# Re-cutting the head of a fused attention and GeGLU kernel: one 256-column part, 512-column dummies, an earlier T3 copy, and later loads for chunk 2

## The chip, the cores and the metric

The kernel runs on one core of a Trainium2 chip. The metric is the device time of one execution in microseconds (us); medians over several executions are quoted.

## The reference

```python
def reference(A_x, A_k_cache, A_v_cache, A_wq, A_wo, B_x, B_w_gate, B_w_up, B_w_down):
    xn = _layernorm(A_x)                       # 2048 x 448, bf16
    q  = xn @ A_wq                             # 16 heads of 256
    p  = softmax(q k^T / 16)                   # last 512 rows of the caches, 8 KV heads
    s  = (p v) @ A_wo
    g  = silu((gelu(xn @ B_w_gate) * (xn @ B_w_up)) @ B_w_down)   # F = 1792
    return A_x + s * g
```

## The kernel before

Each of five engines (PE the matmul engine, ACT, DVE, POOL, and SP for transfers) runs its own list of operations. A semaphore is a counter by which one engine tells another that a step is done; a small planner derives the waits for them. Each matmul is two PE instructions, the load of its weights (PEld in the traces) and the matmul itself, so 9 matmuls fewer are 18 PE instructions fewer. The tokens are handled in chunks of 512 columns; each chunk has four tiles of 128 tokens. A "unit" is one block of 128 columns of the gate and up matrices, for one chunk; it holds two PSUM banks (parts of the memory that PE writes to). The steady loop does two units per step, from unit 4 on.

The head is the part until the loop runs. A tile must be loaded, normalised (statistics on DVE, square root on ACT, scaling on DVE) and transposed on PE into `xnT` before any unit can use it. The first chunk's tiles come one after the other, so the head computes units 0 to 2 in parts of 128 columns, a part for each tile as it arrives.

```python
        warm(19, 2)                 # 19 dummy matmuls of 256 columns, ahead of the first tile
        ln_first(0)                 # statistics and square root
        ln_first(1)
        ln_second(0)                # reciprocal and scaling
        ln_tp_pe(0, ((0, 6), (1, 4)))   # T0: PE transposes of tile 0, copies to xnT by ACT
        warm(2, 2)
        ln_second(1, "act")
        HEAD, PH = (0, 1, 2), (0, 2, 4)
        T = ((None, 6),)
        ln_first(2)                 # on ACT, tile 2's square root stands ahead of T1's copy
        gu_group(HEAD, PH, (0, 1), ((0, 0),))
        ln_tp_pe(1, T)              # T1
        gu_group(HEAD, PH, (0, 1), ((0, 1), 1))
        ...
        ln_tp_pe(2, T)              # T2
        ...
        gu_group(HEAD[:1], PH[:1], (2, 3), (0,))
        ln_a()                      # statistics of tile 4
        ln_tp_pe(3, T, "dve")       # T3, copied by DVE
        ln_a()                      # statistics of tile 5
        ln_b()                      # scaling of tile 4, then its transpose by DMA
        gu_group(HEAD[1:], PH[1:], (2, 3), (0,))
        gu_group(HEAD, PH, (2, 3), (1,))
        gu_group(HEAD[:2], PH[:2], (3, 4))
        for ph in range(2):
            gu_group((3,), (6,), None, (ph,))          # unit 3, all 512 columns
            gu_group(HEAD[2:], PH[2:], (3, 4), (ph,))  # unit 2, last 128 columns
```

`gu_group(units, banks, part, phases)` writes columns `part` (in tiles) of these units. Two matmuls on 64 rows each run side by side, as a pair (in the trace of the kernel before, two of 128 columns start 0.002 to 0.020 us apart and each lasts about 0.22): 8 matmuls in phase 0 and 6 in phase 1 per unit.

The planner orders the waits of an operation by the index of the operation waited for, the largest first; and the emitter issues them in that order ahead of the operation's first instruction.

```python
            for key, d in sorted(want.items(), key=lambda kv: -kv[1].idx):
                ...
                o.waits.append(d)
        ...
    def emit(self, name, eng):
        for o in self.per[name]:
            for d in o.waits:
                eng.wait_ge(...)
            ins = o.fn(eng)
```

The softmax here doesn't subtract the row's maximum and nothing guards it: scores larger than these inputs give would overflow.

## Time and profile before

| kernel before | |
|---|---|
| median of the first 3 runs | 556.48 us (556.04 to 556.8) |
| span of the profiled run | 554.7 us |
| PE busy | 547.6 us, 99% |
| granted PE clock | 1.000 |

The first fence is from the page of the kernel before: the engines' busy times, the queue of instruction transfers (packets, MB, share), and the chain of work that ended last, by engine.

```profile
PE 547.6 (99%) x3626; PEld 260.6 (47%) x3651; DVE 317.1 (57%) x817; ACT 274.1 (49%) x727; POOL 32.9 (6%) x64
...
q8 instruction: 29, 0.48, 0.4%
...
PE 97%; DMA 1%; ACT 1%; issue 0%; DVE 0%; SPq 0%
```

PE is the bound. There is no other engine to relieve, so with the same matmuls time can be won only where PE stands still. The next fence shows where: the busy time of each engine in two stretches of the kernel before (length, then busy us and instructions per engine, granted clock, DMA share, GB/s).

```profile
5.00:14.00 9.00, 8.37 (x220) 6.33 (x220) 7.49 (x23) 5.28 (x12) 1.70 (x4) 1.00 1.09 359
14.00:38.00 24.00, 24.00 (x228) 10.65 (x222) 18.97 (x44) 9.78 (x17) 4.75 (x12) 1.00 0.60 148
```

From 14 to 38 us PE is never idle; before that it is. A matmul's end is modelled in this trace, and matmuls overlap, so the busy time understates small stops. The distance from one matmul's start to the next is the better ruler, and this document uses it: "lost" is that distance less what the same matmuls need where they run without a stop. That need is measured: in the kernel before pairs of 128 columns start 0.056 us apart and pairs of 512 columns 0.216. The 256-column dummies start 0.213 us apart until about 4.8 us, then 0.110. The granted clock of the page does not show this change of pace (`--windows` gives 1.00 from 0 to 5 us too), so "slow" and "fast" pace of PE are read here from the starts alone.

The largest stop is shown by the PE timeline of the kernel before (start, us from first start to last modelled end, tile, shape, count, idle time before it):

```profile
12.25 0.40 PE L328 MATMUL bank<-xnT,wgur 64*128 64x512 bf16 x2
12.47 0.29 PE L328 MATMUL bank<-xnT,wgu 64*128 64x128 bf16 x4
12.99 0.23 PE L328 MATMUL bank<-xnT,wgu 64*128 64x128 bf16 x2 [0.23 <-issue]
13.06 0.22 PE L328 MATMUL bank<-xnT,wgur 64*128 64x128 bf16 x2
```

The lines at 12.47 and 12.99 belong to one group of eight matmuls. By single starts the stop runs from 12.543 to 12.994: 0.451 us where 0.056 is needed, so 0.395 lost. "issue" means that no wait is seen. The matmul after the stop is the 452nd PE instruction in the trace, with weight loads and waits that are instructions of their own counted too; its pair's two weight loads, the 450th and 451st, are held up with it.

These are lines of the engines' timelines of the kernel before, DVE and ACT, then the weight loads that follow:

```profile
6.17 0.63 DVE L376 BATCH_NORM_STATS2 stats<-x 128x6 f32<-128x448 bf16 x1
...
7.05 0.30 ACT L392 ACTIVATE ve<-mv,epst 128x1 f32<-128x1 f32 x1 [0.54 <-DVE mv L379]
7.25 0.58 ACT L322 ACTIVATE xnT<-bank 128x512 bf16<-128x512 bf16 x1
...
7.88 0.17 PEld L328 LDWEIGHTS bank<-xnT,wgu 64*128 64x128 bf16 x6 [0.23 <-ACT xnT L322]
```

ACT takes tile 2's square root (7.05) ahead of T1's copy (7.25), so PE's restart at 7.888 hangs on tile 2's statistics at 6.17, and these on the arrival of tile 2's x, which landed at 6.151. T3's copy stands on DVE behind tile 4's statistics (the first line is their last step):

```profile
10.06 0.18 DVE L379 BATCH_NORM_AGGREGATE mv<-stats 128x2 f32<-128x6 f32 x1
...
10.16 0.39 DVE L438 COPY xnT<-bank 128x512 bf16<-128x512 bf16 x1
```

### The profile page before, as it was taken

The page shows a single profiled execution, that of the slowest core. Times are in us where ns is not written, and L with a number is a line of the kernel's source. Part 1 is how long each engine was busy: PE and PEld are TensorE (multiplying, and loading weights), DVE is VectorE, ACT ScalarE, POOL GpSimd, SP SyncE. Part 2 cuts the span into 40 slices and gives each one's busy share as a digit, 9 for nine tenths or more (in the row PEclk, how much of TensorE's full clock was granted, in tenths as well). Part 3 has the DMA queues.
Part 4 walks back from the last instruction along what each step waited for, and adds up shares of the span by engine and source line. Part 5 has one row for each costly group of instructions (what it writes and reads, how often), then busy time and mean ns, then how long its engine had stood idle before and what let it go on. Part 6 is the DMA issues. An engine that isn't in the chain of part 4 may idle for free.

```text
span 554.7 us, 9768 instructions
## 1 busy us (share of the span) xinstructions
PE 547.6 (99%) x3626; PEld 260.6 (47%) x3651; DVE 317.1 (57%) x817; ACT 274.1 (49%) x727; POOL 32.9 (6%) x64
## 2 busy tenths in 40 slices
PE   8999999999999999999999999999999999999997
PEld 6444444444544444554444444544444454444455
DVE  6783534443385588326588745258747625758722
ACT  5432324353485588205588735058747505758600
POOL 1120830000000000000000000000000000000000
PEclk9999999999999999999999999999999999999999
DMA  9460699401174087413086804147704713807601
GB/s 294 112 164 9 201 283 320 77 1 39 38 133 97 5 152 154 87 35 92 1 151 154 153 1 77 34 106 153 146 11 95 134 34 90 152 20 152 153 8 34
DMA packets 163599, 57.63 MB, mean 104 GB/s; under 512 B 151456, under 2 KB 160672, under 8 KB 163552
## 3 DMA queue, kind: packets, MB, share of 16 engines
q1 hardware_dynamic: 159488, 45.16, 38.7%
q0 software_dynamic: 3296, 11.27, 6.7%
q8 instruction: 29, 0.48, 0.4%
q10 hardware_dynamic: 768, 0.57, 0.3%
q14 instruction: 18, 0.15, 0.1%
HBM read 17.92 MB, written 1.84 MB: 36 GB/s over the span
## 4 chain that ended last, share of the span: by engine, by line
PE 97%; DMA 1%; ACT 1%; issue 0%; DVE 0%; SPq 0%
PE bank L328 97%; DMA x<-in_A_x_dram 1%; ACT qT L322 1%; SPq L316 0%; DVE stats L376 0%; ACT xnT L322 0%; DVE tmp L679 0%; ACT ve L392 0%; DVE ofin L682 0%; PE bank L427 0%; DVE mv L379 0%
## 5 line engine op out<-in xcount | busy, mean ns | idle before, releaser
L641 ACT ACTIVATE p<-bank 128x512 f32<-128x512 f32 x256 | 149.5, 597 | 102.9 <-PE bank L328 100.6
L645 DVE TENSOR_SCALAR pn<-p,rden 128x512 bf16<-128x512 f32 x256 | 124.5, 486 | 16.9 <-DMA pT<-pn 8.1
L328 PE MATMUL bank<-pT,va 128*128 128x512 bf16 x512 | 120.8, 379 | 0.0
L328 PE MATMUL bank<-kT,qT 128*128 128x512 bf16 x487 | 117.8, 379 | 2.0 <-ACT qT L322 1.0
L328 PE MATMUL bank<-wo,oT 128*128 128x448 bf16 (+2 forms) x544 | 97.8, 341 | 0.0
L328 PE MATMUL bank<-xnT,wq 64*128 64x512 bf16 x768 | 94.4, 376 | 0.0
L328 PE MATMUL bank<-xnT,wgu 64*128 64x512 bf16 (+1 forms) x780 | 83.6, 347 | 0.4 <-issue 0.2
L328 PEld LDWEIGHTS bank<-pT,va 128*128 128x128 bf16 x512 | 50.0, 98 | 60.5 <-DMA pT<-pn 0.7
L328 PEld LDWEIGHTS bank<-kT,qT 128*128 128x128 bf16 x512 | 49.6, 98 | 61.2 <-issue 2.5
L328 PEld LDWEIGHTS bank<-wo,oT 128*128 128x128 bf16 x544 | 52.0, 98 | 45.5
L628 DVE CAST qT<-bank 128x512 bf16<-128x512 f32 x64 | 42.9, 692 | 51.0 <-PE bank L328 51.0
L322 ACT ACTIVATE qT<-bank 128x512 bf16<-128x512 f32 x64 | 38.2, 597 | 60.6 <-PE bank L328 59.0
L328 PEld LDWEIGHTS bank<-xnT,wq 64*128 64x128 bf16 x768 | 37.0, 94 | 46.4 <-ACT p L641 1.7
L322 ACT ACTIVATE gl<-bank 128x512 bf16<-128x512 f32 x56 | 33.1, 597 | 49.7 <-PE bank L328 46.5
L495 DVE TENSOR_TENSOR actT<-bank,gl 128x512 bf16<-128x512 f32 x56 | 37.8, 690 | 33.8 <-PE bank L328 25.3
L328 PEld LDWEIGHTS bank<-xnT,wgu 64*128 64x128 bf16 x780 | 35.3, 94 | 39.0 <-issue 1.1
L641 ACT ACTIVATION_READ_ACCUMULATOR p<-bank 128x1 f32 x256 | 52.8, 206 | 0.0
L644 DVE RECIPROCAL rden<-rsum 128x1 f32<-128x1 f32 x256 | 40.4, 158 | 20.3 <-ACT p L641 20.0
L679 DVE SCALAR_TENSOR_TENSOR tmp<-bank,g 128x448 f32<-128x448 f32 (+2 forms) x17 | 10.2, 597 | 71.3 <-PE bank L328 71.3
L664 DVE CAST oT<-bank 128x512 bf16<-128x512 f32 x64 | 43.8, 684 | 6.9 <-PE bank L328 6.9
L328 PE MATMUL bank<-wd,actT 128*128 128x448 bf16 x224 | 43.0, 353 | 0.0
L322 ACT ACTIVATE oT<-bank 128x512 bf16<-128x512 f32 x64 | 39.2, 612 | 7.0 <-PE bank L328 7.0
(39 smaller groups left out, 184.1 us busy)
## 6 DMA issues: line engine op xcount, KB each, us to landing
wo<-in_A_wo_dram POOLq DMA_DIRECT2D x4, 896.0 KB, 18.5
wq<-in_A_wq_dram POOLq DMA_DIRECT2D x2, 1536.0 KB, 10.0
va<-in_A_v_cache_dram POOLq DMA_DIRECT2D x8, 256.0 KB, 13.4
pT<-pn SPq DMA_TRANSPOSE x128, 2.8
xr<-in_A_x_dram POOLq DMA_DIRECT2D x16, 112.0 KB, 2.3
out_dram<-ofin SPq DMA_DIRECT2D x15, 112.0 KB, 1.7
wd<-in_B_w_down_dram SPq DMA_DIRECT2D x1, 1568.0 KB, 7.3
x<-in_A_x_dram SPq DMA_DIRECT2D x2, 448.0 KB, 5.4
```

What stands on the lines that cost most here:

```text
L322: K.op("act", lambda e, o=o, i=i: e.activation(o, i, func, scale=scale), reads, writes)
L328: ins = e.matmul(o, lhsT=l, rhs=r, start=st, stop=sp)
L495: K.op("dve", lambda e: e.tensor_tensor(actT[:, c % 2, f, :], bank[b + 1], gl[:, s, :], ALU.mult), (b_ps[b + 1], b_gl[s]), (b_actT[c % 2][ ...
L628: K.op("dve", lambda v, s=s, b=b: v.tensor_copy(qT[:, s, 1, :], bank[b + 1]), (b_ps[b + 1],), (b_qT[s][1],))
L641: K.op("act", lambda e, b=b, r=r, z=z: e.activation(p32[:, z, :], bank[b], ACT.Exp, scale=att_scale, accum_out=rsum[:, r:r + 1]), (b_ps[b] ...
L644: K.op("dve", lambda e, r=r: e.reciprocal(rden[:, r:r + 1], rsum[:, r:r + 1]), (b_rsum[r],), (b_rden[r],))
L645: K.op("dve", lambda e, r=r, z=z, y=y, t=t4 % 2: e.tensor_scalar(pn[:, y, t, :], p32[:, z, :], rden[:, r:r + 1], None, op0=ALU.mult), (b_p ...
L664: K.op("dve", lambda v, i=i, b=b: v.tensor_copy(oT[:, i, :], bank[b]), (b_ps[b],), (b_oT[i],))
L679: K.op("dve", lambda e: e.scalar_tensor_tensor(out=tmp[:, s, c0:c1], in0=bank[b][:, c0:c1], scalar=0.5, in1=g2[:, t, c0:c1], op0=ALU.mult, ...
```

## The change

The intent can be read from its parts: fewer and longer PE instructions in the head, T3's copy no longer behind tile 4's statistics on DVE, and the work for chunk 2 moved out of the crowded first microseconds. The diff:

```diff
-        load_x("sp", 8, 4)
...
-        def warm(n, b):
+        def warm(n, b, w):
...
-                    ins = e.matmul(bank[b][:, 0:256], lhsT=gl[:, 0, 0:P], rhs=gl[:, 0, 0:256], start=True, stop=True)
+                    ins = e.matmul(bank[b][:, 0:w], lhsT=gl[:, 0, 0:P], rhs=gl[:, 0, 0:w], start=True, stop=True)
...
-        warm(19, 2)
+        warm(9, 2, QC)
+        warm(1, 2, QC // 2)
...
-        ln_a()
         ln_tp_pe(3, T, "dve")
         ln_a()
+        ln_a()
         ln_b()
-        gu_group(HEAD[1:], PH[1:], (2, 3), (0,))
-        gu_group(HEAD, PH, (2, 3), (1,))
+        load_x("sp", 8, 4)
+        gu_group(HEAD[1:2], PH[1:2], (2, 3), (0,))
+        gu_group(HEAD[:2], PH[:2], (2, 3), (1,))
         gu_group(HEAD[:2], PH[:2], (3, 4))
         for ph in range(2):
             gu_group((3,), (6,), None, (ph,))
-            gu_group(HEAD[2:], PH[2:], (3, 4), (ph,))
+            gu_group(HEAD[2:], PH[2:], (2, 4), (ph,))
...
-            ln_a()
+            if ln_t[0] < 8 or n >= 12:
+                ln_a()
```

(`QC` is 512. The second call of `warm`, which now names its unchanged width of 256, is left out.)

More of the change, by code (lines that the diff above doesn't have):

```diff
@@ L536, in bass_recurrent_scan__sliding_block_cached__geglu_ffn__prompt_kernel @@
         ln_tp_pe(0, ((0, 6), (1, 4)))
-        warm(2, 2)
+        warm(2, 2, QC // 2)
         ln_second(1, "act")
```

## The prediction

> **What bounds the kernel.** TensorE. The page gives PE 547.6 us busy of a 554.7 us span (99%) at a granted clock of 1.000; the chain of waits is 97% matmul. In 13 to 37 us the starts of consecutive matmuls show no gap; DVE is about 85% busy there and never holds PE. The change touches only the first 40 us, so only PE gaps in the head (0 to 14 us) can be won. In the timeline, by start-to-start times, they are: cold dummies until 4.8 us, then 5.0 to 5.4 (waiting for the first normalised tile), 0.22 us at 7.7 (T1 copy on ACT), 0.22 at 9.2 (T2 copy on ACT), two of 0.05 at 11.3 and 11.5, and the largest: 12.54 to 12.99, 0.45 where a pair of 128-column matmuls takes 0.055, so 0.40 lost. It falls inside one eight-matmul group, between instructions that wait for no semaphore ("issue"). I read it as instruction starvation. [...] an instruction queue moves 29 packets of 16 KB, the first at 10.4 us lasting 1.2 us, while the DMA engines are full (about 370 GB/s, windows 6 to 12 us) with weights and, from 9.66, the 448 KB of x for chunk 2. About 450 PE instructions lie before the gap.
>
> **What the change does.**
> 1. Dummies: 19 of 256 columns become 9 of 512 plus 1 of 256, the same columns. The starts are 0.213 us apart for 256 columns, so the same 3.9 us, 18 instructions fewer. The next PE work waits for DVE at 5.44 anyway: 0.
> 2. Unit 2: 28 matmuls of 128 columns (about 28 ns each, two row halves overlap) become 14 of 256 (estimate 54 ns, half the 512-column rate of 0.108 us each): 0.78 to 0.76 us, -0.03, and 28 instructions fewer. About 0.39 us of PE work also moves from before units 0/1's last part to after it.
> 3. So that part reaches xnT of tile 3 about 0.39 earlier, near 10.3 us. Its copy, now ahead of tile 4's statistics, can start at about 9.97 instead of 10.16 and end near 10.36. New wait: about +0.1.
> 4. Tile 4's statistics go later, its normalisation (through two POOL operations, about 0.9 us) to about 12.1; the first multiply ends near 13.3 rather than 12.94. PE needs that bank at about 13.6: no wait, but close.
> 5. The 46 instructions saved put the block boundary at the end of the next unit's first phase, about 14.4 us instead of 12.55, and the x load no longer competes with the fetch (it is issued at about 14). Stall gone: -0.40.
> 6. x and LN of chunk 2 later by two loop steps: tiles 8 to 11 are transposed by step 20, needed at 28. Off the path: 0.
>
> Sum: -0.40 - 0.03 + 0.1 = about -0.33 us, 0.06%. Runs of before spread over 0.76 us, so it will hardly show.
>
> **Prediction.** 556.1 us, 8 in 10 between 555.5 and 556.7. Faster by over 2%: 0.005; within 2%: 0.99; slower by over 2%: 0.005.
>
> **What would show it.** The 0.45 us gap at 12.5 gone, first instruction packet at a similar time; a gap of about 0.1 at 10.3 ahead of the (3,4) parts; gelu of unit 0 about 0.3 earlier than 11.54; PE's loop step n=4 starting about 0.35 earlier than 13.9; everything after shifted by that constant.
>
> **What would make it wrong.** The stall isn't instruction fetch, or comes back at the new boundary; the multiply of unit 0 comes so late that PE waits at n=4; [...] moved transposes delay later loads.

The traces show neither how many instructions a block holds nor a release of the clock, only that the dummies' starts go from 0.213 to 0.110 us apart at 4.78 us. "Instruction starvation", "fetch" and "block boundary" are the reading of the stop and of the packets of queue q8; what is measured is the stop's place, at 452 traced PE instructions, and the packets (29 of 16 KB, the first from 10.41 us for 1.24). "Cold" dummies are those that start 0.213 us apart. Read again, the trace of the kernel before gives DVE 78% busy (18.63 of 24.00 us) from 13 to 37 us, not 85%, and 350 GB/s from 6 to 12 us, not 370.

## The result, and the profile after

The changed kernel took 556.47 us (median of 6, 556.19 to 556.67), the kernel before in the same rounds 556.57 (6 runs, 556.0 to 557.05). The ratio is 0.9999, with a 95% interval of 0.9986 to 1.0012. A ratio here is the mean time of one kernel's fast runs over that of the other's of the same rounds, so it is not quite the ratio of the medians.

The page of the changed kernel, the same lines:

```profile
PE 547.6 (99%) x3603; PEld 261.2 (47%) x3628; DVE 317.2 (57%) x817; ACT 273.6 (49%) x727; POOL 32.7 (6%) x64
...
q8 instruction: 29, 0.48, 0.4%
...
PE 98%; DMA 1%; issue 0%; DVE 0%; SPq 0%; ACT 0%
```

The two stretches of the changed kernel, as before:

```profile
5.00:14.00 9.00, 8.40 (x206) 6.37 (x206) 7.30 (x23) 5.22 (x12) 1.57 (x4) 1.00 1.06 359
14.00:38.00 24.00, 24.00 (x228) 12.53 (x222) 16.69 (x37) 9.73 (x17) 3.15 (x8) 1.00 0.55 137
```

DVE has less to do in the second stretch (16.69 us for 18.97, the LN work of chunk 2 comes later) and nothing comes of it, since DVE was not waited for. In the first stretch PE is busy 0.03 us longer. The PE timeline of the changed kernel at the place of the old stop:

```profile
12.34 0.40 PE L328 MATMUL bank<-xnT,wgur 64*128 64x512 bf16 x2
12.55 0.51 PE L328 MATMUL bank<-xnT,wgu 64*128 64x256 bf16 x6
12.88 0.29 PE L328 MATMUL bank<-xnT,wgur 64*128 64x256 bf16 x2
12.99 0.40 PE L328 MATMUL bank<-xnT,wgu 64*128 64x512 bf16 x2
```

The stop is gone, and none has come in its place later. Yet PE reaches this point no sooner. The T1 lines of the changed kernel say where the time went first:

```profile
6.34 0.63 DVE L375 BATCH_NORM_STATS2 stats<-x 128x6 f32<-128x448 bf16 x1 [0.30 <-DMA x<-in_A_x_dram]
...
7.22 0.29 ACT L391 ACTIVATE ve<-mv,epst 128x1 f32<-128x1 f32 x1 [0.76 <-DVE mv L378]
7.42 0.58 ACT L322 ACTIVATE xnT<-bank 128x512 bf16<-128x512 bf16 x1
...
8.11 0.20 PEld L328 LDWEIGHTS bank<-xnT,wgu 64*128 64x128 bf16 x6 [0.52 <-PE bank L328]
```

Tile 2's statistics waited for the transfer of x and began 0.16 us later than in the kernel before. T1's copy is later by the same 0.16, and ends at 7.997; the next matmul starts at 8.142, that is 0.145 after the copy, where it was 0.055 (7.833 to 7.888). Nothing in the diff seems to touch either. T3 is the third place; DVE's copy in the changed kernel, and its statistics of tile 4, now behind:

```profile
10.21 0.42 DVE L437 COPY xnT<-bank 128x512 bf16<-128x512 bf16 x1 [0.56 <-PE bank L426]
...
10.55 0.62 DVE L375 BATCH_NORM_STATS2 stats<-x 128x6 f32<-128x448 bf16 x1
```

The copy ends at 10.638 and PE goes on at 10.785, 0.200 us after its last start where 0.056 is needed; another 0.053 is lost just ahead of it, between the two phases of unit 1. The kernel before lost nothing at T3.

The sum of the starts, in us, against the kernel before:

| term | predicted | first profile after | second profile after |
|---|---|---|---|
| first real matmul | 0 | -0.06 | -0.03 |
| T1's restart | 0 | +0.31 | -0.07 |
| T2's restart | 0 | 0.00 | 0.00 |
| T3's wait, both losses | +0.1 | +0.20 | +0.20 |
| unit 2's matmuls | -0.03 | -0.02 | -0.02 |
| the stop at instruction 452 | -0.40 | -0.40 | -0.40 |
| start of the first down projection | -0.33 | +0.05 | -0.30 |

The last row is read on its own (38.200 us before, 38.252 and 37.899 after); the terms add up to it within 0.02 us. The second profile is the unedited kernel run again, the first experiment below. The start of the first down projection is a good mark, because the rest is nearly fixed: from there to the end ten of the fourteen profiles took 516.43 to 516.51 us, the other four 0.1 to 0.4 more.

So the same kernel shows -0.30 and +0.05. The questions are: what was the stop, what did T1 do, and what is each part of the change worth?

### The profile page after: what moved, and what is told of

The parts are those of the page before. It is cut to its first block, busy times and chain, and to the rows that moved or that the text cites. A ratio compares the mean times of both kernels' runs of the same rounds, so it can differ in the third digit from the quotient of the medians.

```text
span 554.7 us, 9719 instructions
## 1 busy us (share of the span) xinstructions
PE 547.6 (99%) x3603; PEld 261.2 (47%) x3628; DVE 317.2 (57%) x817; ACT 273.6 (49%) x727; POOL 32.7 (6%) x64
## 4 chain that ended last, share of the span: by engine, by line
PE 98%; DMA 1%; issue 0%; DVE 0%; SPq 0%; ACT 0%
PE bank L328 98%; DMA x<-in_A_x_dram 1%; SPq L316 0%; DVE stats L375 0%; ACT xnT L322 0%; DVE tmp L681 0%; ACT ve L391 0%; DVE ofin L684 0%; PE bank L426 0%; DVE mv L378 0%
## 5 line engine op out<-in xcount | busy, mean ns | idle before, releaser
L647 DVE TENSOR_SCALAR pn<-p,rden 128x512 bf16<-128x512 f32 x256 | 124.6, 487 | 14.4 <-DMA pT<-pn 5.4
L328 PE MATMUL bank<-xnT,wgu 64*128 64x512 bf16 (+2 forms) x768 | 83.9, 350 | 0.4 <-ACT xnT L322 0.4
L328 PEld LDWEIGHTS bank<-xnT,wgu 64*128 64x128 bf16 x768 | 36.9, 94 | 37.4 <-issue 0.7
```

What stands on the lines that cost most here:

```text
L328: ins = e.matmul(o, lhsT=l, rhs=r, start=st, stop=sp)
L647: K.op("dve", lambda e, r=r, z=z, y=y, t=t4 % 2: e.tensor_scalar(pn[:, y, t, :], p32[:, z, :], rden[:, r:r + 1], None, op0=ALU.mult), (b_p ...
```

## The experiments

The theories. A: the stop is PE waiting for a block of its own instructions (the first 16 KB packet of the instruction queue q8); it sits at a fixed count of instructions, and moves in the program when instructions are added or removed ahead of it. B: it belongs to unit 2's last part or its banks. C: the load of x for chunk 2 delays the block. D: what the head wins or loses is swallowed later. E: the order of the waits sets the delay of a restart. F: the arrival of tile 2's x sets T1's restart. The kernels go by short names where they are compared: b_ stands for an edit of the kernel before, a_ for one of the changed kernel. The last group (the dummies again, best2, a_best2 and the kernel before again) ran on chip 5, the other experiments on chip 0, so times are compared with the kernel before of the same rounds. All kernels computed the right result.

### The changed kernel again

No edit, timed in 5 rounds.

> The changed kernel, unedited, profiled and timed again beside the next ones. No gap at the old place (about 12.5 us) and none near PE trace instruction 452; about 0.2 us lost ahead of the (3,4) parts (waiting for T3's copy, trace instructions 311 and 323); 0.145 us from the end of T1's copy to the next matmul, as in the first profile. The gap ahead of that matmul changes with the arrival of tile 2's x: each 0.1 us that tile 2's statistics start later than 6.0 us adds about 0.1 us there. Time 556.0 to 556.7, ratio to before 0.999 to 1.0.

Measured: 556.3 us (556.2 to 557.23) against 556.82 before in the same rounds, ratio 0.9994 (0.998 to 1.0008). No stop at instruction 452; 0.053 and 0.143 us lost at T3; 0.145 from T1's copy to the restart. Tile 2's statistics began at 5.99, not 6.34, and T1 lost 0.154, not 0.532. All as expected. The first profile had caught a late x.

### Dummies alone

```diff
-        warm(19, 2)
+        warm([512] * 9 + [256], 2)      # one operation, the same columns
```

> The kernel before with only the dummies changed (one operation of 9 x 512 + 1 x 256 columns, 18 PE instructions fewer, same columns). Theory A (instruction block boundary): the 0.45 us gap inside unit 2's last 128-column part at 12.5 us leaves that place; the boundary comes 18 instructions later, inside unit 3's second phase, about 0.65 us of PE work later, so the gap left there is 0 to 0.2 us and the first down-projection matmul starts at 37.8 to 38.0 us (38.20 before). Theory B (the gap belongs to unit 2's 128-column part or to its banks): the gap stays at that place, 0.40 us lost, down-projection at 38.2. Theory C (the x load of chunk 2 delays the block): like B, or a gap of 0.3 or more at the new boundary.

Measured: no stop anywhere after T2; the down projection starts at 37.646, earlier than I expected, since tile 2 came early (6.02) too. The timeline of PE at the old place, unit 2's last part still in 128 columns:

```profile
12.10 0.40 PE L328 MATMUL bank<-xnT,wgur 64*128 64x512 bf16 x2
12.31 0.35 PE L328 MATMUL bank<-xnT,wgu 64*128 64x128 bf16 x6
12.48 0.24 PE L328 MATMUL bank<-xnT,wgur 64*128 64x128 bf16 x2
```

The same matmuls on the same banks run through. Theory B falls. Removing 18 instructions at the very start of the program cured a stop 11 us later.

> Dummies alone, once more, now timed. Theory A: no gap beyond 0.1 us after T2's restart; the down-projection starts 37.6 to 38.0 us, the spread being tile 2's arrival. Time 0.3 to 0.5 us under before (ratio 0.9992) and 0.1 to 0.2 us under the changed kernel, which pays for T3's wait; less than the interval can show.

Measured: 37.826 us at the down projection, no stop; 556.3 us (555.88 to 556.84) against 556.54, ratio 0.9996 (0.9984 to 1.0009). The trace is as expected; the time is in the expected direction against before but not shown by the interval, and a comparison with the changed kernel was not timed here.

### More instructions ahead of the stop

```diff
-        warm(19, 2)
+        warm([128] * 38, 2)             # the same columns, 38 PE instructions more
```

> The kernel before with 38 dummies of 128 columns, the same columns, 38 PE instructions more. Theory A: the boundary comes 38 instructions earlier, near 11.3 us, and the block still arrives between 12.3 and 13.0 us: a gap of 0.9 to 1.6 us there, none at 12.5; the down-projection starts 0.5 to 1.2 us later than 38.20, and, if the head reaches the end one to one, the kernel takes 0.5 to 1.2 us longer. Theory B: no change, gap at 12.5 as before. Theory D (gains and losses in the head are swallowed later): the head moves, the time does not.

Measured: the stop is again at trace instruction 452, now in an earlier part of the program, and longer: 11.134 to 12.731, 1.541 us lost. The PE timeline of this kernel:

```profile
11.01 0.34 PE L328 MATMUL bank<-xnT,wgu 64*128 64x128 bf16 x6
12.73 0.62 PE L328 MATMUL bank<-xnT,wgu 64*128 64x128 bf16 x8 [1.38 <-issue]
```

Nothing at 12.5. The down projection starts at 39.157, 0.96 us later than before, and the time follows: 557.44 us against 556.73, ratio 1.0021 (1.0007 to 1.0034), which is 0.4 to 1.9 us. Theory A is shown as far as the count goes: all four profiles with the stop have it ahead of the same traced instruction, and 38 PE instructions added ahead of it move it in the program, while 18 removed make it go. That PE waits there for the block in the first packet of queue q8 is inferred (where this document says that the block comes, what was measured is that PE goes on): PE goes on 2.6 to 2.8 us after that packet starts in all four, and of all engines' instructions PE's keep step with q8's 29 packets best: from the start of one packet to that of the next, PE starts 161 to 298 of its 7427 traced instructions in the kernel before (248 on average), DVE 11 to 91 of its 1042. Theory D falls: what the head loses, the kernel loses. PE reached the boundary 1.41 us earlier than in the kernel before, but the block came only 0.26 earlier (12.73 for 12.99). The packet starts at 9.97 to 10.72 us in all fourteen profiles, and at 10.10 in this one, so reaching the boundary earlier mostly lengthens the wait.

### The x load alone

```diff
-        load_x("sp", 8, 4)                      # behind the last weights
...
         ln_b()
+        load_x("sp", 8, 4)
...
-            ln_a()
+            if ln_t[0] < 8 or n >= 12:
+                ln_a()
```

> The kernel before with only the x load of tiles 8 to 11 moved behind tile 4's transpose, and LN of chunk 2 two steps later. Theory A with contention: the block arrives sooner, the gap at 12.5 shrinks from 0.40 lost to under 0.2. Theory A without contention: the gap stays at the same instruction with 0.35 to 0.45 lost. In both no other gap up to 38 us changes by over 0.1 except by the arrival of x.

Measured (one look): the stop stays at instruction 452 with 0.526 us lost, 12.700 to 13.282. Neither expected size (under 0.2, or 0.35 to 0.45) was met.

```profile
12.62 0.29 PE L328 MATMUL bank<-xnT,wgu 64*128 64x128 bf16 x4
13.28 0.23 PE L328 MATMUL bank<-xnT,wgu 64*128 64x128 bf16 x2 [0.37 <-issue]
```

The load's absence did not speed the block up. The packet of the block starts at 10.51 us and lasts 1.21 in this trace, 10.41 and 1.24 in the kernel before: it is not shorter either. Theory C, for this load, finds no support in this one trace; this part of the change is worth nothing that shows. But the edit did not free the DMA engines: their busy share is 1.04 to 1.14 in every microsecond from 8 to 14 here, and 1.06 to 1.12 in the kernel before, filled by weights and x issued earlier. Whether these delay the block was not tested.

### Unit 2's single part, without the earlier T3 copy

```diff
-        gu_group(HEAD[1:], PH[1:], (2, 3), (0,))
-        gu_group(HEAD, PH, (2, 3), (1,))
+        gu_group(HEAD[1:2], PH[1:2], (2, 3), (0,))
+        gu_group(HEAD[:2], PH[:2], (2, 3), (1,))
...
-            gu_group(HEAD[2:], PH[2:], (3, 4), (ph,))
+            gu_group(HEAD[2:], PH[2:], (2, 4), (ph,))
```

> The kernel before with only unit 2's second half as one 256-column part (28 PE instructions fewer ahead of unit 3's end), T3 still evacuated behind tile 4's statistics. Theory A: the gap at 12.5 is gone (boundary about 1 us later). A new wait ahead of the (3,4) part of units 0 and 1, since its tile is wanted about 0.39 us earlier while the copy starts as before at about 10.16: 0.25 to 0.40 us lost. Net on the down-projection: -0.2 to 0.0 us. Theory B in the form that the 128-column part itself is the cause: also gone; in the form of banks: stays.

Measured (one look): no stop at 12.5, and a wait at T3 of 0.217 us with 0.052 ahead of it, 0.27 in sum. The lines of DVE and of the weight load behind it:

```profile
10.35 0.18 DVE L379 BATCH_NORM_AGGREGATE mv<-stats 128x2 f32<-128x6 f32 x1
10.45 0.39 DVE L438 COPY xnT<-bank 128x512 bf16<-128x512 bf16 x1
...
10.90 0.11 PEld L328 LDWEIGHTS bank<-xnT,wgu 64*128 64x128 bf16 x4 [0.23 <-DVE xnT L438]
```

The down projection started at 38.370, later than expected, because this run had the latest tile 2 of all (statistics at 6.47, T1 lost 0.512). So the earlier T3 copy of the full change wins 0.07 of the 0.27 us that the single part costs. It is so little because the restart there comes 0.147 after the copy, and here 0.056: here the wait on DVE stands on the weight load, there in an instruction of its own.

### The order of the waits

In the changed kernel the dummies are two operations of the plan, not one. Every later PE operation then has an index higher by one, and ahead of the matmuls after T1 the planner sorts two waits the other way round.

```diff
 (in the changed kernel)
-        warm(9, 2, QC)
-        warm(1, 2, QC // 2)
+        warm([512] * 9 + [256], 2)
```

> The changed kernel with its ten dummies in one operation, not two; the same instructions but for the order of waits. Theory E (one PE operation more in the plan turns the order of the two waits ahead of the matmuls after T1's copy round, so that the late one stands in an instruction of its own): from the end of T1's copy to the next matmul 0.055 us, as in all variants of before, in place of 0.145; the rest as the changed kernel. Rival: 0.145 stays (it comes of tile 2's late arrival).

Measured (one look): 0.055 us from copy to restart, in place of 0.145. T1's copy and the weight load behind it:

```profile
7.14 0.58 ACT L322 ACTIVATE xnT<-bank 128x512 bf16<-128x512 bf16 x1
...
7.77 0.17 PEld L328 LDWEIGHTS bank<-xnT,wgu 64*128 64x128 bf16 x6 [0.26 <-ACT xnT L322]
```

Theory E is shown. In the trace the wait on ACT then stands on the weight load itself and the wait on PE in a semaphore instruction of its own; in the changed kernel it is the other way round. T2's restart takes 0.144 to 0.146 in every kernel so far, and its wait on ACT stands in an instruction of its own in all of them.

The first try to use this (called best):

```diff
 (in the kernel before, with the dummies as one operation)
-            for d in o.waits:
+            ws = o.waits
+            if name == "pe":
+                ws = sorted(ws, key=lambda d: 0 if d.dma else ("pe", "pool", "dve", "act").index(d.eng) + 1)
+            for d in ws:
```

> The kernel before with 512-column dummies in one operation and, on PE alone, the waits ahead of an instruction put in another order: DMA first, PE's own, then DVE, ACT last, so that the late one rides on the weight load. No fetch gap (-0.40); T2's restart 0.055 after its copy in place of 0.144 (-0.09); the six restarts of the scores after the Q projection 0.06 to 0.08 after ACT's copy in place of 0.168 (-0.5 to -0.6 in sum). Time 0.9 to 1.2 us under before, ratio 0.998, and about 0.8 us under the changed kernel. If the order of waits is nothing, 0.4 under before.

Measured: 556.67 us (556.3 to 557.25) against 556.82, ratio 0.9996 (0.9984 to 1.0009). A miss of mine (0.9 to 1.2 us were expected): T1 now restarts 0.144 after its copy and T2 still 0.144. The trace shows that it is the first wait of the list that goes onto the weight load; I had put the late one last. The edit was turned round (best2):

```diff
+                ws = sorted(ws, key=lambda d: 4 if d.dma else ("act", "dve", "pool", "pe").index(d.eng))
```

> Dummies alone plus the waits of PE in the order opposite to the one in best: ACT first, then DVE, PE's own, DMA last. The traces of best showed that the first wait of the list goes onto the instruction and the rest into instructions of their own, so best had it the wrong way round. Restart 0.055 us after T1's and T2's copies, and 0.06 to 0.09 after ACT's copy at the six starts of scores (0.168 in every run so far): -0.09 at T2 and -0.5 to -0.6 in sum later. Time 0.9 to 1.2 us under before, ratio 0.998. If the six stay at 0.168, the order of waits matters in the head alone.

Measured: T1 and T2 both restart 0.055 to 0.056 us after their copies. The down projection starts at 37.526, the earliest of all. The time is 556.2 us (555.8 to 556.32) against 556.54, ratio 0.9995 (0.9981 to 1.0008): 0.34 us less, not the expected 0.9 to 1.2, and the interval includes 1. The six restarts of the scores did not change, and the reason is a reading error. The page of the kernel before, and that of the same kernel profiled again (below), have these lines:

```profile
L328 PE MATMUL bank<-kT,qT 128*128 128x512 bf16 x487 | 117.8, 379 | 2.0 <-ACT qT L322 1.0
```

```profile
L328 PE MATMUL bank<-kT,qT 128*128 128x512 bf16 x512 | 121.0, 379 | 0.0
```

The program has 512 of these matmuls. In the first trace 25 records are missing, among them the first one of each of the six series. The gap of 0.535 us that I saw holds a matmul without a record, and "waits for ACT" is what the profile makes of it. Where all records are there, the distance is 0.309 with the old order of waits and with the new one. There was nothing to win. The loss goes with the chip: the trace of each kernel profiled on chip 5 has all 512 records, that of each on chip 0 has 487.

The same edits in the changed kernel (a_best2):

> The changed kernel with its dummies in one operation and PE's waits as in best2. T3's restart 0.055 to 0.07 after its copy in place of 0.15. Against best2 it keeps unit 2's single part: -0.03 for the matmuls, and about 0.1 us lost ahead of the (3,4) parts; so 0.05 to 0.1 us later than best2 at the down-projection once tile 2's arrival is taken off. Time 0.8 to 1.1 us under before.

Measured: T2 restarts 0.055 after its copy, T3 0.077. T3's wait costs 0.058 and 0.075 us. The down projection starts at 37.639, 0.113 after best2's, with tile 2 at the same time in both (5.97 and 5.99). The expectation was 0.05 to 0.1 later. 556.16 us (555.91 to 556.42) against 556.54, ratio 0.9994 (0.9982 to 1.0007): 0.38 us less, where 0.8 to 1.1 was expected from the same reading error. So on equal terms unit 2's single part costs about 0.1 us.

### Tile 2's x first

```diff
 (on top of best)
         load_x("sp", 0, 1)
         load_x("act", 1, 1)
+        load_x("sp", 2, 1)
         load_w("sp", 0, 0)
         load_w("act", 0, 1)
-        load_x("sp", 2, 1)
```

> best with tile 2's x issued ahead of the first gate weights on the same queue. Theory F (what varies from run to run in the head is the arrival of tile 2's x): its statistics start before 6.0 us, limited by DVE, and T1's restart loses at most 0.06 us; the times spread less than those of before. Risk: the first weights come 0.1 to 0.3 us later and the first real matmul starts after 6.16. Time within 0.2 us of best, lower if best's runs have a late tile 2.

Measured: tile 2's x lands at 3.80 (6.22 in best), its statistics start at 5.98, and T1 lost 0.068. The first real matmul starts at 6.386, where best has 6.276. 556.54 us (556.21 to 556.77) against 556.82, ratio 0.9992 (0.998 to 1.0005), against best's 0.9996: no difference that shows. In the trace the down projection starts at 37.761, 0.246 before best's. Of the risk named beforehand one half is seen, as the first gate weights land at 6.17 (5.29 in best). That they delayed PE is not shown: the first real matmul starts 0.354 after the last dummy, and in best2 and in the kernel before again, whose gate weights were there by 5.2, it starts 0.353 after it. In all three PE's pace was still slow (the last two dummies, of 256 columns, start 0.188 to 0.189 apart; 0.120 in the first profile of the kernel before).

### The kernel before again

> The kernel before, profiled again. Theory A: 0.35 to 0.65 us lost at PE trace instruction 452, wherever the clock then stands. Theory F: the gap after T1 is 0.06 us when tile 2's statistics start by 6.0 us and grows one to one with a later start.

Measured (one look, on chip 5): the stop is at instruction 452, 12.681 to 12.990, 0.253 us lost, less than the expected 0.35 to 0.65. In this run PE's fast pace came late: pairs of 128 columns are 0.103 apart until about 7.0 us, and 0.056 after it. PE so reached the boundary 0.14 us later than in the first profile, and the block came at the same 12.99. The down projection starts at 38.195, against 38.200. This is an unplanned sign of how the stop works: ahead of it, PE's delays can be free (here 0.14 us), because the block is later still. The block's own arrival is not fixed, though: PE went on at 12.73 to 13.28 in the four profiles with the stop.

T1's restart over all fourteen profiles supports theory F. In eleven of them tile 2's statistics start 0.023 to 0.024 us after its x lands; in the other three x was there earlier. Where the wait on ACT stands on the weight load, PE goes on 1.707 to 1.713 us after the start of tile 2's statistics in nine profiles, whether these start at 5.97 or at 6.47; where it stands apart, after 1.800 to 1.804 in three. The two left over are the run with the late pace and the one with tile 2's x first, in which PE itself was late.

## Why the prediction was right, and where it was not

The class (within 2%) and the range held: 556.47 us in 555.5 to 556.7. But the range holds the kernel before's own 556.57 as well, and a time that no run can tell from before proves no mechanism, so the steps count. Of the marks that the prediction named, the second profile shows the gelu of unit 0 at 11.28 (11.54 before) and the first matmul of unit 4 at 13.615 (13.932 before).

- "Stall gone: -0.40", as instruction starvation at a block boundary: right in the number, -0.40. That the stop keeps to a count of PE instructions is shown by adding 38 (it moves up in the program) and removing 18 (it goes); that the block is what PE waits for is inferred from its packet. Instruction 452 comes at 14.28 and 14.63 us in the two profiles, about where the prediction put the boundary (14.4), and runs through. How many instructions a block holds was not shown. Where the stop occurred it cost 0.25 to 1.54 us.
- "The x load no longer competes with the fetch": wrong as a cause. With the load alone moved, 0.526 us was lost, and other transfers kept the DMA engines full (busy share 1.04 to 1.14).
- Unit 2's matmuls -0.03: right in kind. Pairs of 256 columns start 0.109 to 0.110 apart, which makes about -0.02.
- T3, "about +0.1": mis-sized. It cost 0.053 + 0.144. The copy did start early, as soon as the transposes were done; but the restart took 0.147 after its end, because the late wait stood in an instruction of its own, and a second loss of 0.05 came between the phases of unit 1 when unit 2's matmuls no longer stood between them (argued, not tested; in the trace the weight load there waits for a semaphore of PE's own, raised by the matmul just ahead).
- Dummies "0": right as work, wrong in a side effect. Made as two operations they turned the order of two waits round: +0.09 at T1.
- The first multiply later, "no wait, but close": right; it ends at 13.24 in the second profile (13.3 predicted), and PE shows no stop at unit 4. Chunk 2's LN later, 0: right.
- Not foreseen: T1's restart hangs on tile 2's x. In the kernel before, the block can hide such lateness: in its two profiles T1 restarts at 7.888 and 8.025, and PE goes on after the block at 12.99 in both. In the changed kernel it is not hidden, and it cost 0.16 us in the profile that came first.

The sum of -0.33 was met by the second profile (-0.30) and missed by the first (+0.05). That the two errors (+0.1 at T3, +0.09 at T1) nearly disappear in the second profile is luck in part: tile 2 came early there.

The experiments point to best2, the dummies as one long-column operation and the waits in order, without the rest of the change. Its first down projection starts 0.67 us earlier than before (38.195 on the same chip) and 0.37 earlier than the second profile of the changed kernel (taken on chip 0). Its time ratio to before, 0.9995, has an interval that includes 1, so that it beats either kernel is seen in one trace of its head and not shown by the measured time. The part of the time that stays random lies partly behind the head: the waits of weight loads from 40 us on include, in best2, none on the transposes of the probabilities, and in the kernel with unit 2's single part alone this line:

```profile
PEld bank L328 <- DMA pT<-pn: 1.4, 3, 0.8
```

That kernel's rest took 0.4 us longer than most. What makes these transposes late in some runs stays open. So does why the block takes 2.6 to 2.8 us from the start of its packet until PE goes on, when the packet itself lasts 1.1 to 1.2.

## What to carry to other kernels

A stop in the middle of a group, without any wait, may be the instruction stream: count the instructions ahead of it, add or take away some, and see whether it keeps its count or its place (here it kept traced instruction 452 with 38 more); fewer and longer instructions at the start, 18 fewer already, were the cure here. When a stop that waits for an outside event goes away, delays ahead of it that were free can begin to cost (here 0.16 us at T1), so add up waits in order of time and not one by one. Before you believe a wait that comes back at every repeat, count the records of its group against the program (here 487 of 512).

## What the traces showed besides

- The stop cost 0.253, 0.395, 0.526 and 1.541 us in the four profiles that have it, always at traced instruction 452, in a stretch where PE starts about 58 traced instructions per us (the 165th at 7.611 us, the 449th at 12.543 in the kernel before).
- The step of PE from slow to fast pace varies. In the kernel before it comes 3.6 us after the first dummy; in a_best2 the dummies speed up at about 3.8 us, 2.7 after the first; in best, best2 and best_x2first two dummies at 5.76 to 6.03 us are still slow (0.188 to 0.189 apart), over 4.5 after it; and one run, the kernel before again, took until about 7.0 us, 5.8 after it. What sets it no run shows.
- Of several waits ahead of a matmul, the one on its weight load costs 0.055 to 0.056 us from the end of a copy to the matmul's start, and one in a semaphore instruction of its own 0.144 to 0.147.
- Matmul records can be missing: 487 of 512 turned a distance of 0.309 us into 0.535, put down to ACT, in every profile taken on chip 0 and in none of the four on chip 5. How they were lost no run shows.
